# q loaded as 512-byte runs, early output tiles stored late from eight buffers, layer 1 of two stripes in halves

## The chip, the cores and the metric

The kernel runs on one core of a Trainium2 chip. The metric is the device time of one execution in microseconds (us), less is better. Most executions of one kernel agree within about 1%; a single core's slow executions are those over 1.5% above the fastest of the same kernel, and they are left out of every ratio. Before the change: 226.91 us, median of three runs (225.87 to 227.54).

Engines in the profile: PE is TensorE's matmuls, PEld its weight loads, DVE VectorE, ACT ScalarE, POOL GpSimd, SP SyncE. SPq is SyncE's instruction stream where it issues DMAs; ACTq and POOLq are the same of their engines. A line number such as L386 is a line of the kernel that is profiled: layer 1's matmuls are L332 before and L353 in the changed kernel, layer 2's L365 and L386, the store L374 and L395.

## The reference

Linear attention with a decay per head over 4 batches, 8 heads, 768 tokens of 64 values; its output, 3072 tokens of 512 values, goes through two dense layers (512 to 2048, activation, 2048 to 512).

```python
for b in range(nb):                                   # blocks of 64 tokens
    intra = einsum('bhic,bhjc->bhij', qb, kb) * Dmask
    intra = einsum('bhij,bhjd->bhid', intra, vb)
    inter = einsum('bhid,bhde->bhie', qb * lam_pow, kv_state)
    out[:, :, sl] = intra + inter
    kv_state = lam_block * kv_state + einsum('bhsd,bhse->bhde', kb * rev_pow, vb)
x = out.transpose(0, 2, 1, 3).reshape(3072, 512)
h = x @ w_in
g = where(h >= 1, h, where(h <= -1, 0, (h + 1) ** 2 / 4))
return g @ w_out                                      # 3072 x 512, float32
```

q, k, v, the weights and the output are float32 in memory: 27.3 MB to read, 6.3 MB to write.

## The kernel before

Tokens are handled in 24 chunks of 128 for attention and in 6 stripes of 512 (four chunks) for the dense layers. Every chunk needs one load of q, k and v (256 KB each, token on the partition, eight runs of 256 bytes per partition). A cast multiplies by the decay table and writes bfloat16. From chunk 6 on, k and q are transposed by DMA. Every 128 output tokens are one output tile, copied by ScalarE into a buffer `osb` and stored by one DMA of 128 rows of 2 KB. The program is a list of operations with estimated times and due times, which a small scheduler puts in order for each engine while the kernel is built. Loads of q, k and v, transposes and stores are all issued by SyncE, one after another in the order that the scheduler gave.

```python
LD = 6                                   # buffers of each load
op = tc.tile_pool(name="op", bufs=3)     # output tiles
...
def f_load(c, x, wait):                  # x: 0 q, 1 k, 2 v
    t = ld.tile([128, H, D], F32, ...)
    d = nc.sync.dma_start(out=t, in_=(q, k, v)[x][b, :, s0:s0 + C, :].rearrange("h p d -> p h d"))
...
def cast_v(c):
    nc.scalar.copy(out=v_out(vi[c % NV]), in_=qkv_ld[c, 2]...)
...
def f_x(c):                              # attention's output, transposed, is layer 1's input
    nc.scalar.copy(out=xT[sx][:, :, off:off + C], in_=pot[c])
...
def f_y(s, ms):
    osb[s, ms] = op.tile([128, d_model], F32, name="osb", tag="osb")
    nc.scalar.copy(out=osb[s, ms], in_=py_t[s, ms])
def f_st(s, ms):
    m0 = s * MS + ms * 128
    nc.sync.dma_start(out=out[m0:m0 + 128, :], in_=osb[s, ms])
...
add(("y", y), "ACT", 600, ..., [("l2", n2), ("y", y - 1), ("st", y - 3)])
add(("st", y), "SP", 550, ..., [("y", y), ("st", y - 1)], due=-1, dma=780)   # as soon as it can
```

## Time and profile before

| | before |
|---|---|
| time, median of three | 226.91 us |
| span of the profiled run | 225.5 us |
| TensorE busy | 205.6 us (91%) |
| last transpose of q landed | 158.4 us |
| layer 1 of the last stripe starts | 180.8 us |
| last matmul starts | 221.2 us |

From the page of the profile: the span cut into 40 equal slices of 5.6 us. A digit is the busy share in tenths, PEclk the clock granted to TensorE, DMA the busy share of the 16 DMA engines, GB/s what they moved.

```profile
## 2 busy tenths in 40 slices
PE   0497989999999989689999999999999999999992
...
PEclk9999999999999999999999999999999999999998
DMA  6999999999898797999999999999011001110212
GB/s 121 216 218 170 195 189 202 200 223 196 212 202 158 182 215 169 205 173 204 225 196 237 214 166 233 232 211 211 0 49 47 24 22 49 47 47 16 77 67 77
DMA packets 102837, 34.38 MB, mean 152 GB/s; under 512 B 95136, under 2 KB 99744, under 8 KB 102816
```

TensorE is busy from the second slice to the end. The DMA engines are full until slice 28 (157 us) and nearly idle after it. So there are two limits with little slack: TensorE over all, and DMA for the first 157 us.

The chain of waits that ended last, from the same page, by engine and by line:

```profile
PE 57%; SPq 3%; DMA 2%; issue 1%; ACT 1%; ACTq 0%
PE py L365 27%; PE ph L332 23%; PE po L305 3%; DMA x2f<-in_v_dram 2%; PE ps L285 2%; SPq L406 1%; PE po L302 1%; PE pu L266 1%; SPq L256 1%; SPq L260 1%; ACT vi L235 0%; ACT osb L370 0%; PE pt L285 0%; ACTq L370 0%
```

Over half of the span is TensorE following itself. The matmuls of layer 2 (`py`) and layer 1 (`ph`) are 50% alone.

What engines waited for, with the total, the number of times and the longest, all in us:

```profile
POOL ks L231 <- DMA x1f<-in_k_dram: 48.9, 14, 14.0
...
ACT vi L235 <- DMA x2f<-in_v_dram: 16.4, 13, 3.5
...
PE ph L332 <- ACT xT L312: 1.0, 1, 1.0
```

The DMA issues of q and of the stores: count, KB each, median time from issue to landing.

```profile
x0f<-in_q_dram SPq DMA_DIRECT2D x24, 256.0 KB, 4.4
...
out_dram<-osb SPq DMA_DIRECT2D x24, 256.0 KB, 2.6
```

A store lands 2.6 us after its issue. In the trace's packet records, one that runs alone is 128 packets of 2 KB, 84 to 85 ns each, with 13 in flight at a time, all over in 0.82 us.

### The profile page before, as it was taken

What the parts mean: (1) busy time and instruction counts of PE and PEld (TensorE: products, weight loads), DVE (VectorE), ACT (ScalarE), POOL (GpSimd) and SP (SyncE); (2) the same over time, 40 slices, a digit from 0 to 9 for tenths busy, and PEclk for the clock granted to TensorE, in tenths of its full rate; (3) what the DMA queues carried; (4) which work ended last, traced back from release to release, by engine and by line L of the source; (5) the groups of instructions that cost most, each with busy time, mean ns of one, the idle gap of its engine ahead of it and who ended that gap; (6) DMA issues with size and microseconds to landing.
All of it is one profiled execution on the core that took longest, in us unless ns stands there. A gap on an engine that the chain in (4) does not pass through costs nothing.

```text
span 225.5 us, 4385 instructions
## 1 busy us (share of the span) xinstructions
PE 205.6 (91%) x1733; PEld 123.4 (55%) x1760; DVE 144.2 (64%) x218; ACT 123.6 (55%) x220; POOL 61.0 (27%) x65
## 2 busy tenths in 40 slices
PE   0497989999999989689999999999999999999992
PEld 0376634765888577567664554545545544444441
DVE  7687399978498948567655956856656564554300
ACT  3346867544678285546757575676655444455121
POOL 6543560056034332423342542361000000000000
PEclk9999999999999999999999999999999999999998
DMA  6999999999898797999999999999011001110212
GB/s 121 216 218 170 195 189 202 200 223 196 212 202 158 182 215 169 205 173 204 225 196 237 214 166 233 232 211 211 0 49 47 24 22 49 47 47 16 77 67 77
DMA packets 102837, 34.38 MB, mean 152 GB/s; under 512 B 95136, under 2 KB 99744, under 8 KB 102816
## 3 DMA queue, kind: packets, MB, share of 16 engines
q1 hardware_dynamic: 97920, 29.90, 70.4%
q0 software_dynamic: 4752, 4.19, 12.2%
q8 instruction: 14, 0.23, 0.5%
q14 instruction: 7, 0.06, 0.1%
q10 hardware_dynamic: 144, 0.00, 0.0%
HBM read 27.27 MB, written 6.29 MB: 149 GB/s over the span
## 4 chain that ended last, share of the span: by engine, by line
PE 57%; SPq 3%; DMA 2%; issue 1%; ACT 1%; ACTq 0%
PE py L365 27%; PE ph L332 23%; PE po L305 3%; DMA x2f<-in_v_dram 2%; PE ps L285 2%; SPq L406 1%; PE po L302 1%; PE pu L266 1%; SPq L256 1%; SPq L260 1%; ACT vi L235 0%; ACT osb L370 0%; PE pt L285 0%; ACTq L370 0%
## 5 line engine op out<-in xcount | busy, mean ns | idle before, releaser
L332 PE MATMUL ph<-xT,w_in_sb 128*128 128x128 bf16 (+1 forms) x741 | 92.5, 268 | 1.9 <-ACT xT L312 1.0
L365 PE MATMUL py<-w_out_sb,gT 128*128 128x512 bf16 x368 | 92.6, 379 | 1.0 <-issue 0.2
L340 ACT ACTIVATE r<-ph,one 128x512 bf16<-128x512 f32 (+2 forms) x96 | 64.6, 678 | 47.7 <-PE ph L332 38.4
L332 PEld LDWEIGHTS <-w_in_sb 128*128 128x128 bf16 x752 | 52.5, 98 | 29.0 <-issue 2.2
L365 PEld LDWEIGHTS <-gT 128*128 128x128 bf16 x384 | 35.7, 98 | 38.8 <-DVE gT L356 0.2
L348 DVE TENSOR_SCALAR t<-r 128x1024 bf16<-128x1024 bf16 x48 | 25.2, 526 | 42.7 <-ACT r L340 42.7
L356 DVE TENSOR_TENSOR gT<-w,t 128x1024 bf16<-128x1024 bf16 x48 | 39.8, 828 | 1.6
L231 POOL TENSOR_TENSOR ks<-x1f,tab_k 128x512 bf16<-128x512 f32 x20 | 22.1, 1103 | 62.0 <-DMA x1f<-in_k_dram 48.9
L351 DVE TENSOR_TENSOR w<-r,t 128x1024 bf16<-128x1024 bf16 x48 | 37.2, 775 | 1.5
L231 POOL TENSOR_TENSOR qs<-x0f,tab_q 128x512 bf16<-128x512 f32 x24 | 28.5, 1189 | 25.7 <-DMA x0f<-in_q_dram 25.3
L235 ACT CAST vi<-x2f 128x512 bf16<-128x512 f32 x24 | 14.8, 616 | 16.5 <-DMA x2f<-in_v_dram 16.4
L295 DVE TENSOR_TENSOR sc<-ps,causal 128x512 bf16<-128x512 f32 x20 | 13.8, 689 | 13.6 <-PE pt L285 13.6
L370 ACT COPY osb<-py 128x512 f32<-128x512 f32 x24 | 14.1, 586 | 15.1 <-PE py L365 13.4
L305 PE MATMUL po<-sc,vi 128*128 128x128 bf16 x192 | 19.2, 226 | 0.2
L312 ACT CAST xT<-po 128x512 bf16<-128x512 f32 x24 | 14.0, 585 | 7.2 <-PE po L305 6.6
L270 ACT CAST ubd<-pu 64x256 bf16<-64x256 f32 x40 | 14.6, 364 | 5.3 <-PE pu L266 5.0
L305 PEld LDWEIGHTS <-vi 128*128 128x128 bf16 x192 | 15.2, 102 | 2.3 <-issue 0.6
L302 PE MATMUL po<-qT,ubd 128*128 128x128 bf16 x80 | 15.1, 224 | 0.0
L295 DVE TENSOR_TENSOR sc<-pt,causal 128x512 bf16<-128x512 f32 x20 | 13.6, 680 | 0.0
L266 PE MATMUL pu<-vi,ks 128*128 128x128 bf16 x80 | 8.4, 232 | 2.4 <-ACT vi L235 2.3
L241 PE MATMUL pt<-ident,ks 128*128 128x128 bf16 x24 | 3.1, 266 | 8.0 <-DVE ks L231 7.8
L266 PEld LDWEIGHTS <-ks 128*128 128x128 bf16 x80 | 6.4, 105 | 5.5 <-issue 3.1
(48 smaller groups left out, 87.4 us busy)
## 6 DMA issues: line engine op xcount, KB each, us to landing
x1f<-in_k_dram SPq DMA_DIRECT2D x24, 256.0 KB, 4.8
x0f<-in_q_dram SPq DMA_DIRECT2D x24, 256.0 KB, 4.4
x2f<-in_v_dram SPq DMA_DIRECT2D x24, 256.0 KB, 4.6
out_dram<-osb SPq DMA_DIRECT2D x24, 256.0 KB, 2.6
w_out_sb<-in_moe_w_out_dram POOLq DMA_DIRECT2D x4, 512.0 KB, 13.3
w_in_sb<-in_moe_w_in_dram POOLq DMA_DIRECT2D x3, 512.0 KB, 6.6
w_in_sb<-in_moe_w_in_dram POOLq DMA_DIRECT2D x2, 256.0 KB, 5.0
kT<-ks SPq DMA_TRANSPOSE x18, 4.2
```

What stands on the lines that cost most here:

```text
L231: eng.tensor_tensor(t, qkv_ld[c, x], _bc(tab[:, c % NCB, :], 2, D), op=AX.mult)
L235: nc.scalar.copy(out=v_out(vi[c % NV]), in_=qkv_ld[c, 2].rearrange("p (a b) d -> p a b d", b=2))
L266: nc.tensor.matmul(pu[0][:, hp, :], lhsT=pair(ks[c], hp), rhs=v_pair(vi[c % NV], hp), start=(c % NCB == 0 and hp == 0), stop=True, skip_gr ...
L295: nc.vector.tensor_tensor(sc_sb[c][:, g], pst[c, g], _bc(causal, 1, HP), op=AX.mult)
L302: nc.tensor.matmul(po[:, hp], lhsT=ubd[(c - 1) % NUB][:, hp, :], rhs=qT[c][:, hp, :], start=True, stop=False)
L305: nc.tensor.matmul(po[:, hp], lhsT=vi[c % NV][:, hp, hi].rearrange("p a d -> p (a d)"), rhs=sc_sb[c][:, hi, hp, :], start=(cb == 0 and hi ...
L332: nc.tensor.matmul(ph[:, j * m:(j + 1) * m], lhsT=w_in_sb[:, ko, (ni + j) * 128:(ni + j + 1) * 128], rhs=xT[s][:, ko, part * m:(part + 1) ...
L340: nc.scalar.activation(out=r_t[grp][:, i, cs], in_=ph_t[s, ni, part][:, cs], func=AF.Relu, bias=one[:, 0:1])
L348: nc.vector.tensor_scalar(t_t[grp], r, 0.5, 1.0, op0=AX.mult, op1=AX.min)
L351: nc.vector.tensor_tensor(w_t[grp], r, t_t[grp], op=AX.subtract)
L356: nc.vector.tensor_tensor(gT[s][:, f - RW * n:f, part * m:(part + 1) * m], w_t[grp].rearrange("p a (b m) -> p (a b) m", m=m), t_t[grp].rea ...
L365: nc.tensor.matmul(py_t[s, ms], lhsT=gT[s][:, ko, ms * 128:(ms + 1) * 128], rhs=w_out_sb[:, ko, :], start=(ko == 0), stop=(ko == FO - 1))
```

## The change

Its intent: DMA is full for 157 us, so (1) q is loaded in runs of 512 bytes (two tokens) rather than 256, (2) stores of early tiles are held back until most loads are out, from eight output buffers rather than three, and (3) layer 1 of stripes 3 and 4 is cut into halves of 256 tokens, so that it can start on two chunks.

For (1), a partition now holds two neighbouring tokens for half of the heads: partitions 0 to 63 take heads 0 to 3, partitions 64 to 127 heads 4 to 7, and one q load becomes two DMAs of 64 partitions. After transposing, a chunk's columns come out with all even tokens first, then all odd ones. Nothing sorts them again until the store, whose address pattern puts 64 even rows and 64 odd rows in their places. The diff, cut to its core:

```diff
-    op = ctx.enter_context(tc.tile_pool(name="op", bufs=3))
+    op = ctx.enter_context(tc.tile_pool(name="op", bufs=NO))          # NO = 8
@@ f_load
-        d = nc.sync.dma_start(out=t, in_=(q, k, v)[x][b, :, s0:s0 + C, :].rearrange("h p d -> p h d"))
+        if x == 0:
+            for g in range(2):
+                i = q[b, g * HL:(g + 1) * HL, s0:s0 + C, :].rearrange("l (j e) d -> j l (e d)", e=2)
+                d = nc.sync.dma_start(out=t[64 * g:64 * g + 64].rearrange("p (l e) d -> p l (e d)", e=2), in_=i)
+        else:
+            ...
@@ f_st
-        nc.sync.dma_start(out=out[m0:m0 + 128, :], in_=osb[s, ms])
+        nc.sync.dma_start(out=out[m0:m0 + 128, :].rearrange("(j e) n -> e j n", e=2), in_=osb[s, ms])
@@ schedule
-    QS = (1, 2)
+    PARTS = {1: 4, 2: 4, 3: 2, 4: 2}
...
-            add(("y", y), "ACT", 600, ..., [("l2", n2), ("y", y - 1), ("st", y - 3)])
-            add(("st", y), "SP", 550, ..., due=-1, dma=780)
+            add(("y", y), "ACT", 600, ..., [("l2", n2), ("y", y - 1), ("st", y - NO)])
+            add(("st", y), "SP", 550, ..., due=0.055, dma=780)        # after the first 55 loads
```

(Left out: the tables of powers and the causal mask in the new order of tokens, two more small loads of lam, the q operand of the matmuls taken through a pattern of 2 x 64 columns, and the estimates given to the scheduler.)

## The prediction

> **What bounds it now.** TensorE: busy 205.6 of 225.5 us (the page's engine table). The chain of waits is TensorE from 98.4 to 221.6 us; just before, it runs through DMA (a v load of 5.3 us ending at 97.7, then its cast). By matmul start times TensorE loses 8.7 us before 24 us, 7 us between 24 and 104 us (1.0 at 79, 1.7 at 91.5, 0.7 at 97.8, waiting for xT or v), nothing later, and 4 us of tail. DMA is full until about 157 us (some 200 GB/s in the slices), then nearly idle.
>
> **What the change does.**
> 1. q in 512-byte runs. A load of 1024 packets of 256 B takes 1.14 to 1.2 us when DMA is full, 18.6 ns a packet and engine; a 2 KB packet takes 85 ns. Interpolated (estimate): 28 ns for 512 B, 0.88 us a q load; 24 save about 7 us of DMA time.
> 2. Late stores: six or seven leave the first 95 us.
> 3. Halves: 128 more matmuls of 2.5 ns (estimate), 0.3 us; stripes 3 and 4 start on two chunks, not four.
> 4. Two small lam loads, two iotas, two multiplies: +0.4 us at the start, against 1 us from quicker q.
> If that were all, the 7 us of stalls would go: 218 to 220 us.
>
> **What I think decides.** With q's tokens split even/odd over partitions, the store now writes through a pattern whose slowest dimension is 2 (2 x 64 rows of 2 KB); it was 128 rows. The Trainium skill, "DMA: Bandwidth & Descriptors", section "Why a DMA increments its semaphore by 16 and not by 1", says that a copy is spread over the largest k up to 16 engines that divides the slowest dimension of both sides. Here k = 2. No run shows that yet; before, a quiet store's 128 packets end in 0.82 us (8 per engine of 85 ns). On two engines it is 64 x 85 ns = 5.4 us; 24 stores are 131 us on engines 0 and 1, which also carry a sixteenth of all else: k and v 48 x 1.2 = 58, q 21, transposes about 23, weights 27 us. Sum 260 us, over the present span: two DMA engines bind the kernel.
>
> Queue order (changed program): loads up to chunk 14 go first (about 95 us), then seven stores nearly in a row, 38 us, before chunk 15's v. So TensorE should stand still from about 125 us; later loads queue behind stores too. Last q transpose about 200 us, not 157; layer 1 of stripe 5 begins about 205, not 182; TensorE ends near 245; twelve stores are left after 202 us, 5.4 us each, the last landing near 268.
>
> **Predicted: 266 us, 242 to 286 (8 in 10).** Faster by over 2%: 0.05; within 2%: 0.03; slower by over 2%: 0.92.
>
> **What would show it.** Stores take 7 us or more from issue to landing (median now 2.6), their packets 5 us or more. Mean DMA share low while the chain of waits runs through loads and stores. TensorE idle tens of us between 120 and 210 us; over 15 us of tail after the last matmul. Step 1: 24576 fewer packets under 512 B. Step 3: no visible cost. Stalls at 79 and 91 to 98 us gone or smaller.
>
> **What would make it wrong.** Stores over 16 engines: 216 to 221 us. Two engines alone moving 2 KB packets in 70 ns: about 245. Idle bursts on the two engines: up to 285.

(The 2.5 ns of point 3 comes from the trace of the kernel before: 16 matmuls of 128 columns take 0.89 us in a row, four of 512 columns 0.86 us, so each of the 12 extra ones costs about 2.5 ns, an estimate.)

## The result, and the profile after

The changed kernel took **289.47 us** (median of four, 288.70 to 290.85), beside 227.22 us for the kernel before on the same chip. The ratio is 1.274 [1.264, 1.284]. Here and below, a ratio is the mean time of one kernel's fast runs over the mean of the other's fast runs of the same rounds, so it isn't quite the ratio of the medians; the bracket is a 95% interval. The direction of the prediction was right. Its size was not: 266 us was predicted, and 289.5 lies outside of 242 to 286.

The page after, the same rows as before; a slice is now 7.2 us:

```profile
## 2 busy tenths in 40 slices
PE   0588899996999999200049969971999999999800
...
PEclk9999999999699999955558999997899999999965
DMA  6999999999799992159599964665991111111111
GB/s 132 201 185 195 194 199 207 179 195 163 176 168 165 202 106 67 51 67 90 131 168 93 208 124 99 152 141 116 91 94 54 43 36 36 39 38 39 53 51 41
DMA packets 90758, 34.40 MB, mean 120 GB/s; under 512 B 70768, under 2 KB 87664, under 8 KB 90736
```

DMA is no longer full and then idle. In slices 16 and 17 (108 to 122 us) its share is 2 and 1 tenths, and 1 tenth from slice 31 (215 us) to the end. Two engines of 16 are 0.125. TensorE stands idle in slices 17 to 21 and again at the end, where only stores are left. The clock row falls too, most of all in slices 18 to 21, where TensorE stands idle; a matmul of layer 2 takes a mean of 386 ns for 379 before, so the clock is not what costs the time.

The chain that ended last, and the two DMA issues:

```profile
PE 26%; SPq 8%; DMA 7%; issue 1%; ACT 1%; POOLq 1%; POOL 0%; ACTq 0%
PE py L386 14%; PE ph L353 10%; SPq L429 4%; SPq L431 3%; DMA x2f<-in_v_dram 3%; DMA qT<-qs 3%; DMA x0f<-in_q_dram 1%; ACT r L361 1%; POOLq L568 1%; SPq L395 1%; PE po L326 0%; PE ps L306 0%; PE po L323 0%; ACT osb L391 0%; PE pu L287 0%
```

```profile
x0f<-in_q_dram SPq DMA_DIRECT2D x48, 128.0 KB
...
out_dram<-osb SPq DMA_DIRECT2D x24, 256.0 KB
```

The chain now runs through SyncE's queue (SPq), loads of v and q and transposes of q. The issues have no landing time this time (the profile could not pair their semaphore events), so times of stores are taken from their packets: 128 packets of 2 KB, still 84 ns each in the median, but only **1.9 to 2.1 in flight**, 5.13 us a store where they stand back to back and 6.3 where one runs by itself. The records don't name the DMA engine of a packet; that two engines do the work is read from the packets in flight.

What engines waited for: total, times, longest, all in us.

```profile
POOL ks L246 <- DMA x1f<-in_k_dram: 68.1, 13, 32.7
ACT vi L250 <- DMA x2f<-in_v_dram: 60.3, 16, 30.0
...
PE ph L353 <- ACT xT L333: 31.1, 1, 31.1
...
PE ps L306 <- DMA qT<-qs: 9.3, 3, 6.4
```

TensorE's largest wait is one of 31.1 us, from 116.7 to 147.8 us; the same wait was 1.0 us before. SyncE's issues around it, by start and length:

```profile
104.66 14.69 SPq L395 DMA_DIRECT2D out_dram<-osb  x5
119.46 9.60 SPq L271 DMA_TRANSPOSE kT<-ks  x1
129.16 2.46 SPq L275 DMA_TRANSPOSE qT<-qs  x1
131.72 0.51 SPq L395 DMA_DIRECT2D out_dram<-osb  x1
132.28 2.38 SPq L431 DMA_DIRECT2D x2f<-in_v_dram  x1
134.72 2.55 SPq L431 DMA_DIRECT2D x1f<-in_k_dram  x1
137.31 3.99 SPq L429 DMA_DIRECT2D x0f<-in_q_dram  x2
```

Five stores in a row hold SyncE's queue for 14.7 us, a transpose of k then waits 9.6 us in it, and the load of v of chunk 15 goes out only at 132.28. What became of the marks: last transpose of q issued at 208.8, landed about 213 us (158.4 before); layer 1 of the last stripe starts at 231.2 (180.8); TensorE ends at 271.9 (221.6); 15.3 us of stores follow.

### The profile page after: what moved, and what is told of

It is laid out like the page before. It is cut to its first block, busy times and chain, and to the rows that moved or that the text cites. A ratio compares the mean times of both kernels' runs of the same rounds, so it can differ in the third digit from the quotient of the medians.

```text
span 287.2 us, 4670 instructions
## 1 busy us (share of the span) xinstructions
PE 210.4 (73%) x1859; PEld 139.2 (48%) x1888; DVE 141.7 (49%) x220; ACT 122.8 (43%) x220; POOL 61.2 (21%) x67
## 5 line engine op out<-in xcount | busy, mean ns | idle before, releaser
L353 PE MATMUL ph<-xT,w_in_sb 128*128 128x128 bf16 (+2 forms) x877 | 97.4, 261 | 35.6 <-ACT xT L333 31.1
L353 PEld LDWEIGHTS <-w_in_sb 128*128 128x128 bf16 x880 | 67.9, 101 | 61.3 <-issue 37.6
L369 DVE TENSOR_SCALAR t<-r 128x1024 bf16<-128x1024 bf16 x48 | 25.8, 538 | 75.7 <-ACT r L361 75.7
L306 PE MATMUL ps<-qT,kT 64*128 64x128 bf16 x80 | 8.2, 226 | 9.3 <-DMA qT<-qs 9.3
L306 PEld LDWEIGHTS <-kT 64*128 64x128 bf16 x160 | 5.0, 97 | 13.4 <-DMA kT<-ks 6.6
```

The costliest lines, as they stand in the source:

```text
L353: nc.tensor.matmul(ph[:, j * m:(j + 1) * m], lhsT=w_in_sb[:, ko, (ni + j) * 128:(ni + j + 1) * 128], rhs=xT[s][:, ko, part * m:(part + 1) ...
L369: nc.vector.tensor_scalar(t_t[grp], r, 0.5, 1.0, op0=AX.mult, op1=AX.min)
```

## The experiments

All runs below had three rounds. The kernel before took 226.4 to 229.2 us in the five batches they belong to. "Wrong on purpose" means that data or rows are in the wrong place so that the timing question can be asked; shapes and amounts are kept.

### 1. The store's pattern, undone and alone

Theory: the store's pattern confines it to two DMA engines. Rival: late stores, longer buffers or the q loads do the harm.

`e1_rows` undoes only the pattern in the changed kernel (rows land in the wrong order):

```diff
-  ...out=out[m0:m0 + 128, :].rearrange("(j e) n -> e j n", e=2), in_=osb[s, ms]
+  ...out=out[m0:m0 + 128, :], in_=osb[s, ms]
```

> The changed kernel with one line put back: the store writes 128 rows in a row (slowest dimension 128) instead of 2 x 64. The row order of the result is wrong on purpose; the queue order and every engine's program are the same as in the changed kernel. Theory (the store's pattern puts it on two DMA engines, and that alone is the loss): 216 to 222 us, a store's packets in under 1 us, no long TensorE stall. Rival (the late, bunched stores, the split q loads or the halves lose the time): still above 265 us.

Measured 234.46 us (233.25 to 235.82), ratio to before 1.034 [1.025, 1.043]. 55 of the 62 us are gone, and so is the long stall; a slice is 5.8 us here:

```profile
PE   0287989999967698999949999999999999999993
...
DMA  4999999999879999999999999999311011100212
```

```profile
PE ph L353 <- ACT xT L333: 4.8, 2, 3.1
```

It isn't the 216 to 222 expected: something else in the change costs 3%.

`e2_before_2x64` puts only the pattern into the kernel before (again wrong rows):

> The kernel before with the changed kernel's store pattern alone (2 x 64 rows; row order wrong on purpose), so stores early, three buffers, q in 256-byte runs. Theory (two engines bind): their sum is about 58 + 29 + 23 + 27 + 24 x 5.1 = 260 us, so 262 to 290 us, packets of a store in 5 us or more. Rival (a store of two engines does harm only when seven stand in a row late): below 240 us.

Measured 284.26 us (283.31 to 284.94), ratio 1.251 [1.243, 1.259]. The pattern alone, with three buffers and early stores, makes nearly the whole loss.

### 2. Two correct ways round it

`e3_two_stores` writes each tile by two DMAs of 64 rows:

```diff
+  for e in range(2):
+      nc.sync.dma_start(out=out[m0:m0 + 128, :].rearrange("(j e) n -> e j n", e=2)[e], in_=osb[s, ms][64 * e:64 * e + 64])
```

> The changed kernel with each store as two DMAs of 64 rows (even rows, odd rows), right result. Theory: the slowest dimension is 64, 16 engines again, 217 to 224 us, one more DMA issue of about 0.6 us on the SP queue per tile. Rival (it is the stride of two rows in HBM that is slow, not the number of engines): packets longer than 85 ns or stores still of 5 us, above 260 us.

`e4_xperm` puts the tokens back in order in ScalarE's copy of attention's output, and stores plain rows:

```diff
-  nc.scalar.copy(out=xT[sx][:, :, off:off + C], in_=pot[c])
+  nc.scalar.copy(out=xT[...].rearrange("p k (j e) -> p k e j", e=2), in_=pot[c].rearrange("p k (e j) -> p k e j", e=2))
```

> The changed kernel with the tokens put back in order when x is copied out of PSUM (the ACT copy writes with a step of two), so that the store is the one of before; right result. Theory: as e1_rows, 216 to 223 us; the ACT copy of x no longer than 0.65 us (now 0.585). Rival: above 265 us, or the strided copy costs more than it saves.

Measured: two stores 241.94 us (240.58 to 244.78), 1.063 [1.055, 1.072], its profiled run slow; sorted in the copy 236.15 us (234.79 to 237.14), 1.039 [1.031, 1.047]. Both give the reference's result and take back most of the loss. Neither reached the expectation, nor the kernel before: the same 3% as in `e1_rows` stays, and two stores of half the partitions cost more. The sorted copy of x takes 0.73 us for 0.585, over the 0.65 expected.

### 3. Is it the number of engines, or the stride?

The Trainium skill, "DMA: Bandwidth & Descriptors", section "Why a DMA increments its semaphore by 16 and not by 1", says that the number of engines k is the largest up to 16 that divides the slowest dimension of both sides, and that a DMA issued by SyncE takes the lowest-numbered k. If so, 4 x 32 rows use four engines, 16 x 8 rows use 16, and the stride as such is harmless. Both are the changed kernel with `e=4` or `e=16` in the store (wrong rows).

> The changed kernel with the store's pattern as 4 x 32 rows (row order wrong on purpose), every program otherwise the same. Theory (as many engines as the slowest dimension allows, and the loss is the sum of work on the loaded engines): 4 packets at a time in a store, 2.5 to 2.7 us each; the four engines' sum is about 130 + 24 x 2.6 = 192 us, under the span, so the loss nearly goes: 234 to 242 us, near e1_rows. Rival (any pattern that is not one plain run of rows goes slow, or the loss is proportional to a store's time): 255 us or more.

> The changed kernel with each store's rows grouped 16 x 8 in place of 2 x 64 (rows in the wrong order). Theory (the number of engines is set by the slowest dimension of the store, and the row stride as such is harmless): 232 to 238 us like the store of 128 plain rows (234.5), and about 13 packets in flight. Rival (a strided row pattern is slow in itself, as the 4 x 32 run may suggest): above 250 us.

| rows of a store | packets in flight | one store, back to back | time |
|---|---|---|---|
| 2 x 64 (the change) | 1.9 to 2.1 | 5.13 us | 289.47 |
| 4 x 32 | about 4 | 2.64 us | 266.60 (265.62 to 268.62) |
| 16 x 8 | about 12 | 0.8 to 1.3 us | 238.96 (238.59 to 239.32) |
| 128 (`e1_rows`) | about 13 | 0.8 us | 234.46 |

The packets in flight follow the slowest dimension at every step, and the stride costs little beside it: 16 x 8 is back to 1.048 [1.042, 1.055], one us above its expected range and 4.5 us above `e1_rows` (in another batch). It isn't quite free: a store of 16 x 8 that runs alone takes 1.3 us, one of 128 plain rows 0.83. But the time of 4 x 32 missed its expectation (234 to 242) by 25 us. That expectation took a sum of what an engine has to do; experiment 7 comes back to it.

### 4. What the rest of the change is worth

The 3% in `e1_rows` must be q, the late stores or the halves. Three runs take them apart. `e8_q128x2` is `e1_rows` with each q load cut by heads over all 128 partitions, still in 512-byte runs (wrong data):

```diff
-  for g in range(2):   # 64 partitions, 4 heads each
+  for g in range(2):   # 128 partitions, 2 runs of 512 bytes each
+      i = q[b, 2 * g:2 * g + 2, ...]; i = AP(..., 128 partitions)
+      nc.sync.dma_start(out=t.rearrange("p (l e) d -> p l (e d)", e=2)[:, 2 * g:2 * g + 2], in_=i)
```

> e1_rows with the two q loads of a chunk cut by heads rather than by partitions: each writes 128 partitions in runs of 512 bytes, 256 packets, same bytes, same number of DMAs (wrong data on purpose). Theory ([...]the 512-byte packets run at 140 to 160 GB/s): the q packets' mean time falls from 39 ns to about 28 to 32, the rate while they run is 230 GB/s or more, total 219 to 226 us. Rival (512-byte packets, or two DMAs for one, are slow whatever the partitions; or the late stores and halves lose the time): 232 to 236 us as e1_rows.

`e9_q_halves_256` is the kernel before with q in two DMAs of 64 partitions, 256-byte runs as before (correct):

> The kernel before with each q load cut into two DMAs of 64 partitions, still in 256-byte runs; right result. Theory[...]: q packets slow down, the DMA rate in these stretches falls under 200 GB/s, total 228 to 236 us. Rival (only the 512-byte runs are slow[...]): 226 to 228 us, no slower than before.

`e10_late_halves` is the kernel before with (2) and (3) of the change and nothing else (correct):

> The kernel before with the late stores from eight buffers and the halves of stripes 3 and 4, without the q runs and the store pattern; right result. Theory (those two parts are harmless or help by relieving DMA in the first 100 us): 219 to 226 us. Rival (they, not the q loads, are why e1_rows is 3% slower than before): 230 us or more.

Measured: by heads over 128 partitions 229.71 us (226.69 to 232.36; two of the four runs slow, the profiled one among them), ratio of the two fast runs 1.005 [0.997, 1.013]; halves of 64 partitions in the kernel before 235.96 us (234.96 to 236.92), 1.042 [1.036, 1.047]; late stores and halves alone 226.19 us (225.67 to 227.12), 0.999 [0.994, 1.004].

So the 3% is q, and its cause is the 64 partitions. In the window from 4 to 17 us, where q, k and v are loaded in turn, the columns after the window's length are busy times of PE, PEld, DVE, ACT and POOL with their instructions in brackets, the clock, the DMA share and, last, GB/s. The kernel before, then `e1_rows`, then `e8_q128x2`:

```profile
4.00:17.00 13.00, 7.94 (x64) 6.59 (x65) 9.91 (x21) 5.34 (x13) 6.29 (x6) 1.00 1.32 221
```

```profile
4.00:17.00 13.00, 6.29 (x64) 5.54 (x65) 9.08 (x19) 5.73 (x14) 5.69 (x7) 1.00 1.24 202
```

```profile
4.00:17.00 13.00, 6.26 (x64) 5.46 (x65) 8.08 (x19) 5.62 (x14) 6.71 (x8) 1.00 1.22 232
```

221 GB/s with runs of 256 bytes, 202 with runs of 512 onto 64 partitions, 232 with the same runs onto 128 (in a slow run); `e9_q_halves_256`, 256 bytes onto 64, has 212. Within the window, after its first microsecond, the half-microseconds whose bytes are over nine tenths q move 141 to 157 GB/s onto 64 partitions (three of them) and 229 onto 128 (one). This agrees in kind with the Trainium skill, "SBUF — State Buffer", section "Door 1: The DMA port swizzle", by whose table partitions 0 to 63 reach eight of 16 ports. The longer runs do raise the rate when all partitions take part, though not the kernel's time (1.005), but 128 tokens in pairs fill only 64 partitions for each head, so the change as written has to split them.

The late stores and halves are worth nothing: the load-bound waits they remove (0.97, 1.68 and 0.65 us at 79, 91 and 98 us before) are smaller than the scatter of the runs. The 7 us of stalls that I had counted were partly records that the trace lacks: 27 of 1760 matmuls are missing from it, up to 0.22 us each.

### 5. Four runs on the schedule, and three theories that fell

The mechanism explained the direction, but 289.5 is 23 us above 266. I put that down to the schedule, as TensorE's stall began at 116 us rather than 125 and was 31 us long: ScalarE's order, the five stores in a row, or TensorE's own order.

In the trace ScalarE's copy of x of chunk 13 (147.2 us) stands behind the casts of v of chunks 15 and 16 in its program; the first of the two waits 30.0 us for the load issued at 132.28. `e5_act_order` moves x of two chunks ahead of each cast of v:

```diff
-  ... ("u", c - NV), ("cast", c - 1, 2)]
+  ... ("u", c - NV), ("cast", c - 1, 2), ("x", c - 2)]
```

> The changed kernel (stores on two engines) with one dependency for the ACT queue: the cast of chunk c's v comes after the copy of x of chunk c-2, so the copy that TensorE waits for at 116 us (chunk 13) no longer stands behind the casts of v of chunks 15 and 16, whose loads are held up by the stores. The DMA queue's order is unchanged. Theory (the stall of 31 us is the ACT queue's order on top of the store backlog): the stall at 116 us ends before 125 us, a shorter one of 10 to 20 us comes later, total 265 to 280 us. Rival (the two engines' work alone sets the time; the order only moves the wait): 286 to 292 us as before.

Measured 291.50 us (290.13 to 292.23), 1.286 [1.280, 1.293]. The copy moved to 112.5 us, and ScalarE then waited 30.4 us with the activations behind it; the stall came at 115.9 and lasted 28.8 us. `e16_v_pool` therefore takes the casts of v off ScalarE:

```diff
-  nc.scalar.copy(out=v_out(vi[c % NV]), in_=...)
+  (nc.scalar.copy if c < CPS else nc.gpsimd.tensor_copy)(out=v_out(vi[c % NV]), in_=...)
```

> The changed kernel with the casts of v of chunks 4 and later on GpSimd instead of ScalarE. Theory: the 31 us stall of TensorE from 116 us is ScalarE's in-order queue (the cast of v of chunk 15, whose load was issued behind five stores, stands ahead of the x copy of chunk 13 and of the evictions). Then TensorE runs on at 116 us, a later stall of 10 to 15 us starts near 130 us, layer 1 of stripe 3 starts before 135 us, total 276 to 284 us (the tail of late stores binds then). Rival (the two loaded engines alone set the time, whatever ScalarE waits for): 287 to 292 us.

Measured 292.91 us (290.80 to 295.15), 1.285 [1.274, 1.296]. What TensorE waited for now:

```profile
PE pu L288 <- POOL vi L250: 37.4, 2, 25.5
...
PE ps L307 <- DMA qT<-qs: 12.9, 3, 7.7
```

The stall begins at 121 us, is 25.5 us long and waits for v itself; then TensorE loses 7.7, 11.9 and 3.5 us where it lost 2.7, 1.3 and 6.4. ScalarE's order was not the cause. `e6_early` holds no store back (`due=-1`):

> The changed kernel, with no store held back: the early stores are issued as soon as their tile is done. Theory (the two engines cost per store, bunching costs little): 278 to 290 us. Rival (it is the row of five held stores in the queue that makes the long stall): below 270 us.

Measured 293.40 us (291.60 to 295.99), 1.285 [1.273, 1.296]:

```profile
PE ph L353 <- ACT xT L333: 17.1, 3, 7.2
...
PE ps L306 <- DMA qT<-qs: 12.9, 2, 8.9
```

There is no long stall left, but waits of 2 to 9 us all along from 62 to 195 us. The rival fell, and the measurement is 3 us above my own range. `e13_pe_order` gives TensorE another order, with the attention of chunks 20 to 23 later, so that it does not wait for the last q while layer 1 of stripe 4 could run:

```diff
-    PARTS = {1: 4, 2: 4, 3: 2, 4: 2}
+    PARTS = {1: 4, 2: 4, 3: 2, 4: 2, 5: 1}
```

> The changed kernel with the attention of chunks 20 to 23 due just before layer 1 of stripe 5, so that in TensorE's program stripe 4's layer 1 no longer stands behind scores that wait for a late transposed q. Theory (the time I left out is TensorE's fixed order: about 20 us of stripe 4's work waits behind chunk 20 at 209 us): layer 1 of stripe 5 begins 8 to 18 us earlier than 231 us, total 276 to 284 us. Rival (the two engines alone set the end): 287 to 292 us.

Measured 288.16 us (287.11 to 290.11), 1.264 [1.254, 1.274]; layer 1 of the last stripe at 229.8 us, for 231.2. That theory fell too.

### 6. The q loads with the two engines in place

`e14_q128_2eng` is the changed kernel with q by heads over 128 partitions (wrong data), `e15_both` the same with the other order, `e17_v_pool_q128` with the casts of v on GpSimd.

> The changed kernel (stores on two engines) with the q loads cut by heads, 128 partitions each (wrong data on purpose). Theory (the [...]q loads are a second term that I had with the wrong sign): 5 to 9 us quicker, 280 to 285 us; the first store issue and chunk 15's v 3 to 5 us earlier. Rival (once two engines bind, other DMA time does not show): 288 to 291 us.

> e13 and e14 together. Theory (these two are what the prediction missed by): 268 to 277 us, near the predicted 266. Rival: no better than the better of the two.

> As the run before, and q loaded by heads over 128 partitions in place of two DMAs of 64 partitions (wrong data on purpose). Theory: both mis-sized terms of the prediction are taken out, so 268 to 276 us, near the predicted 266. Rival (only the q loads matter): near 282 us, as the run with the q loads alone.

Measured: 281.83 us (281.36 to 282.84), 1.236 [1.227, 1.244]; 278.43 us (277.46 to 282.63, profiled run slow), 1.219 [1.209, 1.228]; 283.27 us (282.62 to 283.95), 1.242 [1.233, 1.251]. The q loads are worth about 8 us of the 23 (289.5 to 281.8, in different batches; 292.9 to 283.3 with the casts of v on GpSimd, in one batch). The second is just outside of its range; it is 3.4 us below the first in the same batch, so TensorE's order does count for a little there. The third is what the rival said: nothing comes from ScalarE's order.

### 7. All stores behind all loads

By now five schedules of the changed kernel took 288 to 293 us. The theory that was left: the two engines are the limit by their sum, whatever the order. Then TensorE's stalls are only the place where the schedule lets the wait show. `e20_all_last` removes every stall by issuing no store before the last load and transpose:

```diff
-    NO = 8
+    NO = 18
-  ... [("y", y), ("st", y - 1)], due=0.055, dma=780)
+  ... [("y", y), ("st", y - 1), ("ld", NCH - 1, 2), ("qT", NCH - 1), ("t", NCH - 1)], due=0.055, dma=780)
```

> The changed kernel with 18 output buffers and every store issued after the last load and transpose: no store stands among the loads. Theory (the two engines are the limit by their sum, and TensorE's stalls only follow from where the stores are put): loads end near 156 to 162 us, TensorE has no stall after 60 us above 5 us and ends at 222 to 230 us, and yet the total stays at 278 to 290 us, as 24 stores of 5.1 us (123 us) follow the loads. Rival (TensorE's 31 us stall and what follows from it is the loss): below 265 us.

`e21_all_last_4x32` is the same with stores of 4 x 32 rows (wrong rows):

> The same with the stores as 4 x 32 rows (rows in the wrong order). Theory: 24 stores of 2.6 us (63 us) after 158 us are done near 221 us, under TensorE's end, so 226 to 234 us, where the same stores among the loads took 266.6 us. Rival (a store over four engines is slow in itself, 4.3 us as some of that run's stores were): 24 of 4.3 us, 258 to 266 us.

Measured: 2 x 64 rows, correct, **289.88 us** (288.54 to 291.31), 1.278 [1.270, 1.285]; 4 x 32 rows 235.49 us (235.20 to 235.58), 1.036 [1.033, 1.039]. The slices of the first of the two (7.2 us each), and its stores by the same profile (length of the issue in ns, min/median/max, first and last start in us):

```profile
PE   0688899996999989999999999999999300000000
...
DMA  6999999999999999999945211111111111111111
GB/s 135 200 182 199 202 200 207 176 194 166 182 171 178 173 204 160 173 202 201 182 94 93 56 51 54 51 55 51 51 51 54 51 51 51 51 51 51 51 51 41
```

```profile
L395 SPq DMA_DIRECT2D out_dram<-osb x24: 537/4948/7149, 159.9 to 267.2; - x24
```

TensorE is busy from slice 2 to slice 31 and starts its last matmul at 224.2 us, 3 us after the kernel before. After the first 24 us it waits once for more than 2 us (2.5 us for a transpose of q at 68). And the time is the same as that of the changed kernel, in which TensorE stood still for over 40 us. The first store starts at 161.2 us; 24 follow one another every 5.126 us, the sum of 123 us, to 285.5. An issue of a store takes a median of 4.9 us, close to the 5.13 us of a store: SyncE seems to be held up by the stores before it (inferred).

With four engines in the same place, the 24 stores take 2.6 us each and end with TensorE:

```profile
PE   0287979999967699989999999999999999999970
...
DMA  5999999999889999999999999356222222222221
GB/s 118 213 208 167 200 192 199 205 207 154 188 158 143 182 182 181 181 181 195 158 156 197 222 178 166 87 104 80 61 105 103 102 102 105 102 102 100 71 73 59
```

That is 31 us less than the same stores among the loads (266.6). So `e7_4x32` was not slow in itself. Four engines have 161 + 24 x 2.6 = 224 us of work, about TensorE's end, so there the order does count; with two engines it moved the time by some 5 us at most (288.2 to 293.4). The result is 1.5 us above its expected range, as the last four stores, which wait for TensorE, took 3.5 to 4.2 us.

That `e20_all_last` and the changed kernel agree to 0.4 us is partly chance. In the changed kernel the last packets of loads and transposes ended at 212.7 us with twelve stores done, 10 us sooner than 161 + 12 x 5.13 = 222.6 us. Its last twelve stores then took 73.2 us instead of 61.6: from 230.7 us on, five of them wait for TensorE's tiles and run alone, 6.3 us each. So the sum of the two engines holds to within about 10 us.

## Why the prediction was right and wrong

**Right: the mechanism.** "Here k = 2" and "two DMA engines bind the kernel". Two packets are in flight, undoing the pattern takes 55 us back, the pattern alone costs 57 us, and stores of four and 16 groups have the packets in flight that the rule says, nearly. "On two engines it is 64 x 85 ns = 5.4 us" was 5.1 to 6.6 us. The order of the queue was right too: seven stores were issued from 98.7 to 131.7 us, before chunk 15's v at 132.3.

**Wrong: one term of the sum.** The step that failed is "k and v 48 x 1.2 = 58, q 21, transposes about 23, weights 27 us. Sum 260 us". I put the loads' share of the two engines at 129 us. With no store among them, the loads and transposes last until 161 us (`e20_all_last`), 32 us more; the stores' own 131 us were 123. 161 + 123 = 284 us, span 286.8, time 289.9. Not all of the 161 us need be work of the two engines: in the changed kernel loads, transposes and twelve stores were done by 212.7 us, which leaves at most 212.7 - 12 x 5.13 = 151 us for the loads (an estimate), 22 us over my 129; another 8 us of its miss are the last twelve stores, 73.2 us for 12 x 5.4 = 65. Of the 32 us, about 8 are shown to be q. Step 1, "24 save about 7 us of DMA time", had the wrong sign, because I interpolated the packet's duration from its size alone and did not ask how many partitions it goes to. For the other 24 us there is only arithmetic: I took every transfer at its best. 1.2 us for 256 KB is 218 GB/s, while the first 20 slices of `e20_all_last` average 184 GB/s; 129 us scaled by 218 over 184 are 153 us, q's slowness and the ramp at the start (135 GB/s) included, and the thin end (94 and 93 GB/s in slices 21 and 22) accounts for the rest: the last load is issued at 143.9 us, and the last eight transposes go out from 148.6 to 159.8 us. This split is an estimate, not tested by a run of its own.

**Wrong, but not the cause: the timetable.** "TensorE should stand still from about 125 us", layer 1 of stripe 5 "about 205", TensorE's end "near 245". Measured: 117, 231 and 272 us. I took this for the reason of the miss and built three theories on it. The runs moved the stalls and left the time: 291.5, 292.9, 293.4 and 288.2 us, and 289.9 with hardly any stall. When one resource is busy nearly all the time, the rest of the schedule mostly decides who is seen waiting for it.

**Right: the signs.** 24368 fewer packets under 512 bytes (24576 predicted); a mean of 120 GB/s for 152; a tail of 15.3 us after TensorE (over 15 predicted); TensorE idle for tens of us between 120 and 210. The stores' time to landing can't be checked, as the profile gives none.

**Wrong: "218 to 220 us" for the rest of the change.** Late stores and halves alone are 0.999 of before. The stalls that they remove were smaller than I had read from a trace with missing records.

No kernel here beats the one before beyond the noise. The closest are `e10_late_halves` (0.999) and, with wrong data, `e8_q128x2` (1.005).

**Open.** How the 24 us of load time divides between k and v, transposes and waits for buffers; and why a store that runs alone on two engines takes 6.3 us and one in a row 5.13. The packets narrow the last one down: in such a store 110 of the 128 packets take 84 ns as well, while 14 to 16, all among the first 48, take from over 100 to 453 ns. Stores of 4 x 32 and 16 x 8 rows that run alone start slowly too, those of 128 plain rows don't (packets of 82 to 89 ns).

## What to carry to other kernels

Reading or writing rows in a regrouped order can be free in bytes and still cost a quarter of the time: look at the slowest dimension of each side of a DMA before anything else, and keep the 128 partitions there. When a few engines carry extra work, add up all that they carry, at the rate that the loads really had over the whole phase and not at their best, and compare the sum with the span before looking at any stall; here such a sum was good to about 10 us. To test such a sum, move the suspected work to where nothing can wait for it: if the time stays, the stalls were a symptom; check then, as above, that it does not stay by chance.

## What the Trainium skill lacked or had wrong

- "DMA: Bandwidth & Descriptors", section "Why a DMA increments its semaphore by 16 and not by 1": its rule for k held in all four patterns as far as packets in flight show it (2, 4, about 12 and 13). It gives no time for a small k: a store of 128 x 2 KB took 0.82 us alone on 16 engines, 2.6 on four and 5.13 on two in a row, and as such stores ran one after another, never two side by side, 24 of them added 123 us after the last load.
- The same page, section "Specifications", gives 512 bytes as the least transfer for line rate. Here 512-byte runs onto 64 partitions were slower than 256-byte runs onto 128 (202 and 221 GB/s from 4 to 17 us); onto 128 partitions they were faster (232). The row should name the partitions beside the run.
- The same page, section "Rules for kernel authors", says of two transfers to disjoint partition halves "Don't bother — they serialize". The runs don't show the two halves one after another, but they show a price that the row doesn't give: q in two halves of 64 partitions made the kernel before 1.042 times as long.
- The page's section "Specifications" gives about 27 GiB/s per engine. Two engines with nothing but stores of 2 KB packets moved 256 KB in 5.126 us, 51 GB/s, which is 25.6 GB/s (23.8 GiB/s) an engine.
- "SBUF — State Buffer", section "Door 1: The DMA port swizzle": by its table 64 partitions in a row reach half of the ports, and it measured 196 GB/s onto 64 partitions and 328 onto 128 with 1 MiB a DMA. It has no figures for DMAs of 128 KB in 512-byte runs: here 141 to 157 GB/s onto 64 partitions and 229 onto 128, about the same ratio.
